# Attention and feed-forward of one kernel interleaved by 256 tokens, on one core

## The chip, the core and the metric

The kernel runs on one core of one Trainium2 chip. The metric is device time in microseconds (us); lower is better. A kernel is executed several times, and medians of its runs are quoted. All runs in this document are of the fast, undisturbed state. The span in a profile is the time from the first to the last instruction of one profiled execution; it is about 2 us shorter than the device time of the same execution.

Names used below: TensorE is PE in the profile (PEld is its weight load), VectorE is DVE, ScalarE is ACT, GpSimd is POOL, SyncE is SP. L289 means line 289 of that kernel's file. PSUM is the accumulator memory that TensorE writes. The granted clock is the share of TensorE's full clock that was let through, as the trace records it. An engine's issue is the distance from the start of one of its instructions to the start of the next.

## The reference, cut to what matters

```
# attention: q, k, v are (4 batches, 8 heads, 768 tokens, 64)
scores = (1 / sqrt(64)) * q @ k.T
scores = where(mask, scores, -1e9)        # blocks of 32: neighbours, first and last block, 3 sampled blocks
attn   = exp(scores - max) / (sum + 1e-9)
x      = attn @ v                         # reordered to 3072 tokens x 512
# feed-forward
h    = x @ w_in                           # 512 -> 1024
e    = exp(h - max);  solu = h * e / (sum(e) + 1e-9)
ln   = (solu - mean) / sqrt(var + 1e-6) * g_ln
out  = ln @ w_out                         # 1024 -> 512
```

Two facts of algebra carry the change. The output of a layer norm does not change (up to the epsilon) when its input is scaled, so the division by the sum of e can be dropped and put into the epsilon (the kernel before does this already). And "subtract the mean, multiply by g, multiply by w_out" is linear, so the subtraction can be folded into the weights once: centred w_out = g * w_out minus the mean of each of its columns. The row factor 1/sqrt(var) can then wait until the output.

## The kernel before

It has two phases. The first does attention, one (batch, head) after the other, and writes x to DRAM. The second reads x back, 128 tokens at a time, and does the feed-forward.

Attention: one head is transposed at a time (64 rows of a 128-row array), scores of 256 columns are collected in tiles of 1536, and ScalarE takes one exponential of each tile.

```
def load_bh_tp(a_tp, bi, qc, kc):
    for src, dst in ((kc, kT), (qc, qT)):
        tp = a_tp.tile([D, S], BF16, tag="tp")
        for c in range(NCH):                                   # 6 transposes of 128 x 64
            nc.tensor.matmul(tp[:, c * TQ : (c + 1) * TQ], src[:, c, :], ident, is_transpose=True, ...)
        nc.vector.tensor_copy(out=dst[0:D, :], in_=tp)
...
    for jh in range(NCH // NJG):                               # 3 tiles a head
        sco = a_sco.tile([TQ, NJG, NSUB, 256], FP32, tag="sco")
        emit_score(jh, qT, kT, sco)                            # 6 matmuls of 256 columns
        if op is not None:
            emit_out(jh, prev_exs, prev_vaug, op, ...)         # attention times v of the head before
        nc.scalar.activation(out=exs[...], in_=sco, func=ACT.Exp, scale=scale)
...
    for ic in range(NCH):                                      # x goes to DRAM
        nc.sync.dma_start(out=x_slabs[b * NCH + ic][:, h * D : (h + 1) * D], in_=o[:, ic, :])
```

Feed-forward, for each 128 tokens:

```
nc.sync.dma_start(out=xt, in_=x_slabs[t])
# 4 transposes of xt into PSUM, then
nc.scalar.copy(out=xT, in_=tps)
# 8 matmuls of 512 columns: hps = x @ w_in
nc.scalar.activation(out=e, in_=hps, func=ACT.Exp, scale=1.0, accum_out=esum)
nc.vector.tensor_mul(out=solu, in0=hps, in1=e)
# bn_stats, bn_aggr: mean and variance; vpe = esum * esum * eps + variance
nc.scalar.activation(out=rstd, in_=vpe, func=ACT.Ln)
nc.scalar.activation(out=rstd, in_=rstd, func=ACT.Exp, scale=-0.5)
nc.vector.tensor_scalar(out=ln, in0=solu, scalar1=mv[:, 0:1], scalar2=rstd, op0=ALU.subtract, op1=ALU.mult)
# 8 transposes of ln into PSUM, then
nc.scalar.copy(out=lnT, in_=tps2)
# 8 matmuls of 512 columns: ops = ln @ w_out
nc.scalar.copy(out=ot, in_=ops)
nc.sync.dma_start(out=out[t * 128 : (t + 1) * 128, :], in_=ot)
```

The softmax here doesn't subtract the row's maximum and nothing guards it: scores larger than these inputs give would overflow.

## Time and profile before

| | before |
|---|---|
| time | 366.1 us median of 4 runs (363.5 to 367.3) |
| attention | about 26 to 177 us; one head takes 4.66 us; its three exponentials of 1.45 us, which overlap a little, keep ScalarE busy for 4.13 us of it (89%) |
| gap between the phases | 177 to 189.5 us |
| feed-forward | 189.5 to 364 us; one tile of 128 tokens takes about 7.3 us |
| ScalarE busy | 277.8 us (76%) |
| TensorE busy | 267.2 us (73%) |

The page of the kernel before, busy time by engine, then the span in 40 slices (a digit is the busy share of a slice in tenths, PEclk the granted clock of TensorE in tenths):

```profile
PE 267.2 (73%) x2772; PEld 180.5 (50%) x2785; DVE 147.3 (40%) x355; ACT 277.8 (76%) x314; POOL 82.8 (23%) x110
...
PE   0049999999999999999356679766867575767654
...
ACT  1018988888888888888429998798878868967883
...
PEclk9999999999999999999769988989898899869888
```

From slice 4 to 19 TensorE is at 9 tenths and ScalarE at 8 to 9. Then comes a hole of one slice, where everything waits for x to go through DRAM. In the second half TensorE is half to three quarters busy, ScalarE is the fuller engine, and the clock is below full.

The page of the kernel before, groups of instructions (busy us, mean ns of one | idle time before them and what ended it):

```profile
L232 ACT ACTIVATE exs<-sco 128x1536 bf16<-128x1536 f32 x96 | 132.4, 1451 | 41.1 <-PE sco L175 41.1
...
L153 PE MATMUL tp<-ident,kc 128*64 128x128 bf16 x192 | 17.5, 229 | 18.9 <-DMA kc<-in_k_dram 18.9
L289 ACT ACT_TABLE_LOAD x24 | 30.8, 1283 | 0.4
...
L290 ACT ACT_TABLE_LOAD x18 | 23.1, 1283 | 0.3
```

Ln and exponential alternate in the feed-forward, and each alternation loads ScalarE's function table again, at 1283 ns. With 6 more before the large exponential there are 48 loads in the second phase, 48 x 1.283 = 61.6 us; one more loads the first table at the very start. The timeline of ScalarE in one feed-forward tile of the kernel before shows them standing right between the work (start, duration):

```profile
302.30 0.58 ACT L264 COPY xT<-tps 128x512 bf16<-128x512 bf16 x1
302.89 1.28 ACT L289 ACT_TABLE_LOAD   x1
304.19 0.20 ACT L289 ACTIVATE rstd<-vpe 128x1 f32<-128x1 f32 x1
304.30 0.57 ACT L264 COPY xT<-tps 128x512 bf16<-128x512 bf16 x1
304.88 1.28 ACT L290 ACT_TABLE_LOAD   x1
306.18 0.20 ACT L290 ACTIVATE rstd<-rstd 128x1 f32<-128x1 f32 x1
```

An activation of 0.20 us costs 1.48 us each time.

The timeline of TensorE in the attention of the kernel before gives the prices that the prediction uses:

```profile
101.16 1.47 PE L175 MATMUL sco<-qT_0_60,kT_0_62 128*128 128x256 bf16 x12
102.47 0.53 PE L185 MATMUL op<-vaug,exs 128*128 128x65 bf16 x12
102.92 0.52 PE L153 MATMUL tp<-ident,kc 128*64 128x128 bf16 x6
```

Twelve matmuls of 256 columns in 1.47 us, of which the last takes 0.27 by itself, are 109 ns from start to start; transposes come out at about 58 ns, attention times v at about 31 ns.

### The profile page before, as it was taken

What the parts mean: (1) busy time and instruction counts of PE and PEld (TensorE: products, weight loads), DVE (VectorE), ACT (ScalarE), POOL (GpSimd) and SP (SyncE); (2) the same over time, 40 slices, a digit from 0 to 9 for tenths busy, and PEclk for the clock granted to TensorE, in tenths of its full rate; (3) what the DMA queues carried; (4) which work ended last, traced back from release to release, by engine and by line L of the source; (5) the groups of instructions that cost most, each with busy time, mean ns of one, the idle gap of its engine ahead of it and who ended that gap; (6) DMA issues with size and microseconds to landing.
All of it is one profiled execution on the core that took longest, in us unless ns stands there. A gap on an engine that the chain in (4) does not pass through costs nothing.

```text
span 364.2 us, 6988 instructions
## 1 busy us (share of the span) xinstructions
PE 267.2 (73%) x2772; PEld 180.5 (50%) x2785; DVE 147.3 (40%) x355; ACT 277.8 (76%) x314; POOL 82.8 (23%) x110
## 2 busy tenths in 40 slices
PE   0049999999999999999356679766867575767654
PEld 0037878888878788888233234333323332323221
DVE  5413343333433343343108454453542615614450
ACT  1018988888888888888429998798878868967883
POOL 4096555555555455510000000000000000000000
PEclk9999999999999999999769988989898899869888
DMA  6699999999999999961121012211120111101011
GB/s 203 143 102 93 86 86 86 85 83 89 88 88 87 86 86 84 89 55 23 23 74 58 31 45 74 98 46 49 66 77 11 58 58 58 46 29 59 12 47 58
DMA packets 112467, 25.64 MB, mean 70 GB/s; under 512 B 104753, under 2 KB 107826, under 8 KB 112434
## 3 DMA queue, kind: packets, MB, share of 16 engines
q0 software_dynamic: 75792, 10.49, 42.2%
q1 hardware_dynamic: 36642, 14.70, 17.6%
q8 instruction: 22, 0.36, 0.4%
q14 instruction: 11, 0.09, 0.1%
HBM read 26.22 MB, written 9.44 MB: 98 GB/s over the span
## 4 chain that ended last, share of the span: by engine, by line
ACT 37%; PE 33%; DVE 10%; DMA 8%; issue 8%; SPq 2%; POOL 0%; ACTq 0%; DVEq 0%
PE sco L175 13%; ACT exs L232 12%; ACT L289 7%; PE ops L303 7%; ACT lnT L300 5%; ACT e L274 4%; PE tp L153 4%; DMA w_out_f<-in_moe_w_out_dram 3%; PE op L185 3%; ACT xT L264 2%; ACT L290 2%; DVE qT_1_61 L156 2%; PE hps L267 2%; PE hps L269 2%; DVE qT_0_60 L156 2%
## 5 line engine op out<-in xcount | busy, mean ns | idle before, releaser
L232 ACT ACTIVATE exs<-sco 128x1536 bf16<-128x1536 f32 x96 | 132.4, 1451 | 41.1 <-PE sco L175 41.1
L303 PE MATMUL ops<-w_out_sb,lnT 128*128 128x512 bf16 x186 | 54.2, 440 | 15.6 <-ACT lnT L300 15.1
L185 PE MATMUL op<-vaug,exs 128*128 128x65 bf16 x1152 | 51.5, 194 | 1.4 <-ACT exs L232 1.2
L277 DVE TENSOR_TENSOR solu<-hps,e 128x1024 bf16<-128x1024 f32 x24 | 29.0, 1210 | 55.8 <-ACT e L274 55.8
L185 PEld LDWEIGHTS <-exs 128*128 128x128 bf16 x1152 | 45.1, 98 | 7.0 <-ACT exs L232 1.5
L267 PE MATMUL hps<-w_in_sb,xT 128*128 128x512 bf16 x94 | 39.6, 421 | 7.1 <-ACT xT L264 6.7
L303 PEld LDWEIGHTS <-lnT 128*128 128x128 bf16 x192 | 19.2, 109 | 47.1 <-ACT lnT L300 23.1
L175 PE MATMUL sco<-qT_0_60,kT_0_62 128*128 128x256 bf16 x288 | 37.8, 278 | 4.6 <-DVE qT_0_60 L156 0.6
L175 PE MATMUL sco<-qT_1_61,kT_1_63 128*128 128x256 bf16 x288 | 36.7, 272 | 4.8 <-ACT exs L232 0.6
L269 PE MATMUL hps<-w_in_sb,xT 128*128 128x512 bf16 x91 | 37.3, 410 | 0.8 <-ACT xT L264 0.8
L141 POOL DMA_DIRECT2D vaug<-in_v_dram x32 | 26.5, 828 | 49.0 <-PE op L185 41.5
L175 PEld LDWEIGHTS <-kT_0_62 128*128 128x128 bf16 x288 | 28.4, 99 | 10.4 <-issue 4.4
L175 PEld LDWEIGHTS <-kT_1_63 128*128 128x128 bf16 x288 | 27.8, 97 | 10.1 <-issue 4.4
L297 PEld LDWEIGHTS <-ln 128*128 128x128 bf16 x192 | 13.1, 107 | 39.3 <-DVE ln L292 36.7
L138 POOL DMA_DIRECT2D qc<-in_q_dram x32 | 26.6, 831 | 24.9 <-PE tp L153 11.9
L153 PE MATMUL tp<-ident,kc 128*64 128x128 bf16 x192 | 17.5, 229 | 18.9 <-DMA kc<-in_k_dram 18.9
L289 ACT ACT_TABLE_LOAD x24 | 30.8, 1283 | 0.4
L292 DVE TENSOR_SCALAR ln<-solu,mv,rstd 128x1024 bf16<-128x1024 bf16 x24 | 13.1, 544 | 42.4 <-ACT rstd L290 42.4
L274 ACT ACTIVATE e<-hps 128x1024 bf16<-128x1024 f32 x24 | 24.6, 1027 | 5.4 <-PE hps L269 5.0
L139 POOL DMA_DIRECT2D kc<-in_k_dram x32 | 26.7, 840 | 0.8 <-PE tp L153 0.6
L306 ACT COPY ot<-ops 128x512 f32<-128x512 f32 x24 | 13.9, 578 | 12.6 <-PE ops L303 12.6
L290 ACT ACT_TABLE_LOAD x18 | 23.1, 1283 | 0.3
(110 smaller groups left out, 276.5 us busy)
## 6 DMA issues: line engine op xcount, KB each, us to landing
out_dram<-ot SPq DMA_DIRECT2D x24, 256.0 KB, 2.0
qc<-in_q_dram POOLq DMA_DIRECT2D x32, 96.0 KB, 3.5
kc<-in_k_dram POOLq DMA_DIRECT2D x32, 96.0 KB, 3.6
vaug<-in_v_dram POOLq DMA_DIRECT2D x32, 96.0 KB, 3.2
w_out_f<-in_moe_w_out_dram SPq DMA_DIRECT2D x1, 2048.0 KB, 11.2
w_in_sb<-in_moe_w_in_dram POOLq DMA_DIRECT2D x1, 1024.0 KB, 10.7
xslab_123<-o SPq DMA_DIRECT2D x8, 16.0 KB, 2.2
xslab_124<-o SPq DMA_DIRECT2D x8, 16.0 KB, 2.5
```

Of the source, the lines that this page charges most:

```text
L139: nc.gpsimd.dma_start(out=kc, in_=k[b, h, :, :].rearrange("(c p) d -> p c d", p=TQ))
L153: nc.tensor.matmul(tp[:, c * TQ : (c + 1) * TQ], src[:, c, :], ident, is_transpose=True, start=(c == 0), stop=(c == NCH - 1))
L175: nc.tensor.matmul(sco[:, jj, c, :], kT[:, jc * TQ : (jc + 1) * TQ], qT[:, c * 256 : (c + 1) * 256], start=(ci % 2 == 0), stop=(ci % 2 == 1))
L185: nc.tensor.matmul(op[:, ic, :], exs[:, jc, ic * TQ : (ic + 1) * TQ], vaug[:, jc, :], start=first, stop=(last and jj == NJG - 1 and ic == ...
L232: nc.scalar.activation(out=exs[:, jh * NJG : (jh + 1) * NJG, :].rearrange("p j (s x) -> p j s x", x=256), in_=sco, func=ACT.Exp, scale=scale)
L267: nc.tensor.matmul(hps[:, 0:512], xT[:, c, :], w_in_sb[:, c, 0:512], start=(c == 0), stop=(c == KD - 1))
L269: nc.tensor.matmul(hps[:, 512:1024], xT[:, c, :], w_in_sb[:, c, 512:1024], start=(c == 0), stop=(c == KD - 1))
L274: nc.scalar.activation(out=e, in_=hps, func=ACT.Exp, scale=1.0, accum_out=esum)
L277: nc.vector.tensor_mul(out=solu, in0=hps, in1=e)
L289: nc.scalar.activation(out=rstd, in_=vpe, func=ACT.Ln)
L290: nc.scalar.activation(out=rstd, in_=rstd, func=ACT.Exp, scale=-0.5)
L303: nc.tensor.matmul(ops, lnT[:, c, :], w_out_sb[:, c, :], start=(c == 0), stop=(c == KF - 1))
```

## The change

The intent is to give ScalarE less to do and to let TensorE work through ScalarE's exponentials. Attention is emitted for 256 queries and all heads, in 12 groups; the feed-forward of one group is cut into pieces that are emitted between the scores of the next group. x stays in SBUF. The feed-forward is transposed: its hidden dimension lies on the partitions, so ln need not be transposed. In both kernels the mask enters the scores as 24 extra rows of the transposed q and k (the mask rows). The sums over the hidden dimension, which now runs over partitions, become one-column matmuls with a vector of ones. The centring is in the weights, the reciprocal square root is a power on GpSimd, and q and k are transposed two heads at a time. The diff, cut to its core:

```diff
-            nc.sync.dma_start(out=xt, in_=x_slabs[t])
-            nc.scalar.copy(out=xT, in_=tps)
+                nc.vector.tensor_copy(out=xT[:, :, qt * P : (qt + 1) * P], in_=tps)
...
-                nc.tensor.matmul(hps[:, 0:512], xT[:, c, :], w_in_sb[:, c, 0:512], ...)
+                    nc.tensor.matmul(h[:, ff, :], w_in_sb[:, c, f * P : (f + 1) * P],
+                                     st["xT"][:, c, :], ...)                     # 32 of 256 columns
+            nc.scalar.activation(out=st["e"][:, sl, :], in_=h, func=ACT.Exp)       # 512 columns
+            nc.vector.tensor_mul(out=st["solu"][:, sl, :], in0=h, in1=st["e"][:, sl, :])
+            nc.vector.tensor_mul(out=st["sq"][:, sl, :], in0=st["solu"][:, sl, :], in1=st["solu"][:, sl, :])
...
-            nc.vector.bn_stats(...); nc.vector.bn_aggr(...)
+                for g, nm in enumerate(("e", "solu", "sq")):
+                    for f in range(KF):
+                        nc.tensor.matmul(s3p[:, qt, g : g + 1],
+                                         st[nm][:, f, qt * P : (qt + 1) * P], onesf[:, 0:1], ...)
...
-            nc.scalar.activation(out=rstd, in_=vpe, func=ACT.Ln)
-            nc.scalar.activation(out=rstd, in_=rstd, func=ACT.Exp, scale=-0.5)
+            nc.gpsimd.tensor_tensor(out=rs, in0=v2, in1=neg_half, op=ALU.pow)
...
-            # ln, 8 transposes of ln, nc.scalar.copy(out=lnT, in_=tps2)
+                nc.tensor.matmul(ops, st["solu"][:, f, qt * P : (qt + 1) * P], w_out_sb[:, f, :], ...)
...
+    def prep_w1():                                       # once, in the first group
+        for c in range(KF):
+            nc.vector.tensor_scalar(out=w_out_g[:, c, :], in0=w_out_f[:, c, :], scalar1=g_sb[:, c : c + 1], ...)
+    def prep_w2():
+        for c in range(KF):
+            nc.tensor.matmul(cs, onesf, w_out_g[:, c, :], ...)
+        nc.scalar.mul(out=wbar, in_=cs, mul=1.0 / d_ff)
+        for c in range(KF):
+            nc.vector.scalar_tensor_tensor(out=w_out_sb[:, c, :], in0=w_out_f[:, c, :],
+                scalar=g_sb[:, c : c + 1], in1=wbar, op0=ALU.mult, op1=ALU.subtract)
...
+    for u, (b, t, pr) in enumerate(units):               # batch, 256 queries, pair of heads
+        for n in range(3):
+            scores(b, t, pr, n, exs)                     # 4 matmuls of 256 columns, exponential of 1024
+            if n == 0 and prev is not None:
+                pv(pb, pt, ppr, pexs, xs[(pb, pt)])      # attention times v of the pair before
+                if ppr == NPR - 1:
+                    bg.extend(ffn_pieces(pb, pt, xs[(pb, pt)]))
+            if bg:
+                bg.popleft()()                           # one piece of background work
```

## The prediction

> **What bounds the kernel now.** The kernel has two phases. By the table of stretches, attention runs from about 25 to 175 us, then the feed-forward from 183 to 364 us; the start is long because the first q/k load waits for w_out scaling (chain of waits: w_out DMA, scaling, load at 17.5 us; first exponential 26.4 us). In attention one head takes 4.66 us, of which ScalarE computes 3 exponentials of 1.45 us: ScalarE bound, 94%. In the feed-forward one 128-token tile takes about 7.5 us and ScalarE is 80-85% busy: exponential 1.03, PSUM copies 0.59, 1.01 and 0.58, and about two table loads of 1.28 us each. TensorE there is busy 70%, at a granted clock near 0.9.
>
> **What the change removes.** All 48 table loads but one (62 us), lnT and xT copies (38 us), half of the output copies (7 us) leave ScalarE; also the 192 transposes of ln, half of the q/k transposes, x's trip through DRAM, bn_stats and the ln pass.
>
> **What it adds.** 576 one-column matmuls for the sums; squares and xT copies on VectorE; mask DMAs at the start; w_out centring once. The attention exponentials become 144 of 1024 columns; 1451 ns at 1536 and 1027 ns at 1024 columns give 0.83 ns a column and 0.18 us fixed, so 148 us instead of 132. Feed-forward exponentials of 512 columns: 48 x 0.60 = 29 us; half of the output 7 us. ScalarE total about 185 us instead of 278.
>
> **New bound: TensorE issue.** Distances between starts read from the timeline of attention: 256 columns 109 ns (12 in 1.47 us), attention-times-v 31 ns, transposes 58 ns, 512 columns 217 ns. The Trainium skill, "TensorE: Matmul & The Clock Gate", section "Back-to-back issue gap", gives N/2.4 + 2.5 ns, 109 ns for 256: this trace agrees. The sums I take at 31 ns too, an estimate (same page: never below about 25 ns). Per group of 256 tokens: scores 48 x 109 = 5.2; a.v 96 x 31 = 3.0; h 32 x 109 = 3.5; sums 1.5; output 16 x 217 = 3.5; x transposes 0.5; q/k transposes 0.9 on average: 18.1 us, against 15.3 us of ScalarE. Eight of twelve slots carry feed-forward work and are TensorE bound, four are exponential bound: 18.6 us, with the coupling loss of 5% seen now T = 19.5 us per group; VectorE needs about 12 us.
>
> **Time.** First exponential about 20 us (VectorE: memsets, mask, copies in order). The first group has no feed-forward but VectorE is loaded with transposes' copies and 16 w_out operations: ends near 39 us. 11 groups x 19.5 = 214. The last feed-forward runs alone: about 11 us. Sum 264 us; range 247 to 284. Faster by over 2%: 0.98; within 2%: 0.015; slower: 0.005.
>
> **What would show it.** One table load; ScalarE busy about 185 us (70%); TensorE clock near 1.0 in the middle and its busy tenths all 9; distance of group starts 19-20 us; waits of exponentials for scores where feed-forward runs; one-column matmuls every 25-35 ns; the chain mostly TensorE lines (scores, h, output, sums).
>
> **What would make it wrong.** One-column matmuls at 60 ns or more (+1.5 us per group, +16 us); GpSimd's power chain being slow, holding the two-buffer PSUM pool (+1-2 us per group); GpSimd loads blocking that chain; a start longer than 25 us from VectorE or mask DMAs; or better overlap than assumed, T near 18 us (248 us).

## The result, and the profile after

Ratios here and below are the mean time of one kernel's fast runs over the mean time of the kernel before's fast runs of the same rounds, so they are not quite the ratio of the medians that stand beside them.

| | before | after |
|---|---|---|
| time, median | 366.1 us | 281.95 us (281.8 to 282.8, 4 runs) |
| ratio | | 0.772, 95% interval 0.769 to 0.775 |
| ScalarE busy | 277.8 us | 174.4 us (62%) |
| TensorE busy | 267.2 us | 238.8 us (85%) |
| table loads | 49 | 1 |
| mean granted clock | 0.932 | 0.997 |

The change takes 84 us off. The predicted 264 us is 18 us below the result; the result lies inside the range, near its upper end.

The page of the kernel after, in the same order as before:

```profile
PE 238.8 (85%) x3163; PEld 183.2 (65%) x3177; DVE 157.9 (56%) x365; ACT 174.4 (62%) x206; POOL 82.8 (29%) x142
...
PE   0116686999999999999999999999999999899783
...
ACT  1002468548858859667677688588488595785630
...
PEclk9999999999999999999999999999999999999998
```

From slice 8 on, up to the last slices, TensorE is at 9 of 10 almost without a break; ScalarE is at 4 to 9. The engines have changed places. Beyond that, two things stand out: the first seven slices, about 50 us, are not full, and neither are the last three.

The timeline of TensorE in the steady part of the kernel after:

```profile
170.12 1.91 PE L268 MATMUL h<-xT,w_in_sb 128*128 128x256 bf16 x16
...
177.13 0.34 PE L283 MATMUL s3p<-onesf,e 128*128 128x1 bf16 x8
...
178.12 1.89 PE L304 MATMUL ops<-w_out_sb,solu 128*128 128x512 bf16 x7
...
182.34 0.50 PE L161 MATMUL tp<-ident,kc 128*128 128x128 bf16 x6
```

Eight one-column matmuls take 0.34 us, of which the last is 0.164 by itself: (0.34 - 0.164) / 7 = 25 ns from start to start. The Trainium skill, "TensorE: Matmul & The Clock Gate", section "Wait — 56ns, not 53.3ns?", says that start-to-start never goes below about 25 ns, however few the columns; this trace agrees, and the 31 ns of the prediction were a little too careful.

The timeline of ScalarE in the kernel after, the first feed-forward exponential of the first two groups and of the last two:

```profile
52.83 0.60 ACT L272 ACTIVATE e<-h 128x512 bf16<-128x512 f32 x1 [0.36 <-PE h L268]
...
72.30 0.60 ACT L272 ACTIVATE e<-h 128x512 bf16<-128x512 f32 x1 [0.43 <-PE h L268]
...
249.73 1.30 ACT L272 ACTIVATE e<-h 128x512 bf16<-128x512 f32 x2
...
268.44 0.60 ACT L272 ACTIVATE e<-h 128x512 bf16<-128x512 f32 x1 [3.36 <-PE h L268]
```

From 52.83 to 249.73 there are ten groups, so one takes 19.7 us. The prediction said 19.5. What is wrong lies outside: the first group and the last.

To see the first group, read VectorE, which works through its queue in order. That order is the compiled one and not quite that of the program: the copies into va_92, the v of the second batch, belong to later units than the w_out work and still stand ahead of part of it. The timeline of VectorE in the kernel after, some lines up to the first feed-forward work (in brackets, the idle time before and what ended it):

```profile
15.27 0.63 DVE L167 COPY va_91<-vc 128x768 bf16<-128x768 bf16 x1 [11.16 <-DMA vc<-in_v_dram]
...
34.14 3.80 DVE L192 TENSOR_SCALAR w_out_g<-w_out_f,g_sb 128x512 bf16<-128x512 f32 x8
...
42.49 0.52 DVE L167 COPY va_92<-vc 128x768 bf16<-128x768 bf16 x1 [0.93 <-DMA vc<-in_v_dram]
42.93 5.37 DVE L203 SCALAR_TENSOR_TENSOR w_out_sb<-w_out_f,g_sb,wbar 128x512 bf16<-128x512 f32 x8
...
48.55 0.76 DVE L240 TENSOR_TENSOR x<-op,r 128x256 bf16<-128x256 f32 x2
...
50.19 0.42 DVE L240 TENSOR_TENSOR x<-op,r 128x256 bf16<-128x256 f32 x1
```

VectorE waits 11.16 us for the first v although the work on the mask, which the first scores need, stands behind that copy. Later a copy of the second batch's v and the 9.2 us on w_out (3.80 + 5.37) stand ahead of the norms of the first group (the divisions that write x), which end at 50.6 us. The first batch's own last data, the v of its fourth pair, had landed at 32.2 us; from 20 to 50 us VectorE is busy for 26.2 of the 30 us (table of stretches).

The timeline of TensorE in the kernel after, the same instructions early and a little later:

```profile
24.37 0.80 PE L161 MATMUL tp<-ident,qc 128*128 128x128 bf16 x6 [1.53 <-DVE qT_87 L166]
...
34.19 1.53 PE L231 MATMUL op<-va_91,ex 128*128 128x65 bf16 x24
...
38.98 0.49 PE L161 MATMUL tp<-ident,qc 128*128 128x128 bf16 x6
...
41.29 0.91 PE L231 MATMUL op<-va_91,ex 128*128 128x65 bf16 x24
```

Until about 36 us the same six transposes take 0.80 us instead of 0.49, and the same 24 matmuls 1.53 us instead of 0.91: TensorE runs at about half rate up to then. The prediction did not count this either.

The last group's feed-forward has no attention beside it to hide in. The timeline of all engines at the end of the kernel after:

```profile
265.81 0.42 DVE L240 TENSOR_TENSOR x<-op,r 128x256 bf16<-128x256 f32 x1
...
267.37 1.91 PE L268 MATMUL h<-xT,w_in_sb 128*128 128x256 bf16 x16 [0.62 <-DVE xT L258]
...
274.87 0.17 DVE L290 TENSOR_TENSOR s_4734<-s3p,st_sel 128x6 f32<-128x6 f32 x1 [1.07 <-PE s3p L283]
...
275.93 0.69 POOL L298 TENSOR_TENSOR rs<-v_4738,neg_half 128x2 f32<-128x2 f32 x1
...
277.15 0.69 ACT L312 ACTIVATE ot<-ops,rs 128x512 f32<-128x512 f32 x1 [4.53 <-PE ops L304]
```

From the last division, which ends at 266.2 us, to the end at 281.1 us there are 14.9 us: 1.2 us for transposing x, 7.5 us for h, exponentials, products and sums in turns, 1.8 us up to the end of the power, 1.2 us up to the end of the last output tile, and 3.3 us until it has left.

### The profile page after: what moved, and what is told of

The parts are those of the page before. It is cut to its first block, busy times and chain, and to the rows that moved or that the text cites. A ratio compares the mean times of both kernels' runs of the same rounds, so it can differ in the third digit from the quotient of the medians.

```text
span 281.1 us, 7445 instructions
## 1 busy us (share of the span) xinstructions
PE 238.8 (85%) x3163; PEld 183.2 (65%) x3177; DVE 157.9 (56%) x365; ACT 174.4 (62%) x206; POOL 82.8 (29%) x142
## 2 busy tenths in 40 slices
DMA packets 61636, 20.40 MB, mean 73 GB/s; under 512 B 52225, under 2 KB 56994, under 8 KB 61602
## 4 chain that ended last, share of the span: by engine, by line
PE 62%; DMA 11%; ACT 10%; DVE 9%; issue 3%; POOL 3%; ACTq 0%; POOLq 0%
PE s L215 15%; PE h L268 15%; PE ops L304 14%; PE op L231 10%; ACT ex L220 8%; DMA kc<-in_k_dram 7%; PE s3p L283 6%; DMA vc<-in_v_dram 4%; DVE w_out_sb L203 2%; ACT ot L312 2%; PE tp L161 2%; POOL qc L73 1%; DVE xT L258 1%; PE tps L256 1%; DVE x L240 1%
## 5 line engine op out<-in xcount | busy, mean ns | idle before, releaser
L220 ACT ACTIVATE ex<-s 128x1024 bf16<-128x1024 f32 x144 | 141.1, 1024 | 68.9 <-PE s L215 67.8
L215 PE MATMUL s<-qT_87,kT_85 88*128 88x256 bf16 (+1 forms) x288 | 49.5, 284 | 5.8 <-ACT ex L220 3.1
L231 PEld LDWEIGHTS <-ex 128*128 128x128 bf16 x1152 | 45.7, 98 | 11.1 <-ACT ex L220 4.6
L268 PE MATMUL h<-xT,w_in_sb 128*128 128x256 bf16 x384 | 47.8, 272 | 1.3 <-DVE xT L258 0.6
L215 PE MATMUL s<-qT_88,kT_86 88*128 88x256 bf16 (+1 forms) x288 | 46.2, 272 | 2.0 <-ACT ex L220 1.2
L273 DVE TENSOR_TENSOR solu<-h,e 128x512 bf16<-128x512 f32 x48 | 33.0, 687 | 26.3 <-ACT e L272 26.2
L304 PE MATMUL ops<-w_out_sb,solu 128*128 128x512 bf16 x179 | 44.6, 378 | 0.9 <-DVE s_4734 L290 0.3
L268 PEld LDWEIGHTS <-w_in_sb 128*128 128x128 bf16 x384 | 37.0, 97 | 6.3 <-issue 1.6
L272 ACT ACTIVATE e<-h 128x512 bf16<-128x512 f32 x48 | 28.7, 598 | 18.1 <-PE h L268 16.9
L215 PEld LDWEIGHTS <-kT_85 88*128 88x128 bf16 (+1 forms) x288 | 27.3, 101 | 13.5 <-issue 6.0
L215 PEld LDWEIGHTS <-kT_86 88*128 88x128 bf16 (+1 forms) x288 | 26.0, 97 | 9.3 <-issue 4.0
L73 POOL DMA_DIRECT2D qc<-in_q_dram x32 | 26.2, 822 | 8.0 <-DMA w_in_sb<-in_moe_w_in_dram 3.7
L231 PE MATMUL op<-va_92,ex 128*128 128x65 bf16 x576 | 26.2, 193 | 2.7 <-ACT ex L220 2.2
L231 PE MATMUL op<-va_91,ex 128*128 128x65 bf16 x576 | 25.2, 196 | 1.9 <-DVE x L240 1.0
L274 DVE TENSOR_TENSOR sq<-solu 128x512 bf16<-128x512 bf16 x48 | 20.4, 425 | 1.3
```

The source lines that it names most:

```text
L73: nc.gpsimd.dma_start(out=t[:, :, hh, :], in_=src[b, 2 * pr + hh, :, :].rearrange("(p c) d -> p c d", p=P))
L215: nc.tensor.matmul(s[:, m, :], kT[i][rows[hh], hh, pr, jc * P : (jc + 1) * P], qT[i][rows[hh], hh, pr, t * TW : (t + 1) * TW], start=(m % ...
L220: nc.scalar.activation(out=e, in_=s, func=ACT.Exp, scale=scale)
L231: nc.tensor.matmul(op[:, qt, hh, :], exs[n][:, m, qt * P : (qt + 1) * P], va[i][:, 2 * pr + hh, jc, :], start=first, stop=(n == 2 and m == ...
L268: nc.tensor.matmul(h[:, ff, :], w_in_sb[:, c, f * P : (f + 1) * P], st["xT"][:, c, :], start=(ff == 0 and c == 0), stop=(ff == 1 and c == ...
L272: nc.scalar.activation(out=st["e"][:, sl, :], in_=h, func=ACT.Exp)
```

## The experiments

All runs but one gave correct results. Each was run in three rounds against the kernel before.

### Where the 84 us came from

**e1: the kernel before without table switches.** Only the Ln and the exponential of the reciprocal root are replaced by a power on GpSimd.

```diff
-            nc.scalar.activation(out=rstd, in_=vpe, func=ACT.Ln)
-            nc.scalar.activation(out=rstd, in_=rstd, func=ACT.Exp, scale=-0.5)
+            nc.gpsimd.tensor_tensor(out=rstd, in0=vpe, in1=neg_half, op=ALU.pow)
```

> The kernel before with one edit: the reciprocal root of the variance is taken by GpSimd's power instruction instead of ScalarE's logarithm and exponential, so that no activation table is switched. Theory A (the table switches, 48 of 1.28 us in ScalarE's stream, are the largest single part of the feed-forward phase): one 128-token tile falls from 7.5 us to about 5 us, where TensorE (about 4.2 us of issue) takes over; total about 306 us. Rival B (the feed-forward phase is bound by the chain through four engines and by the TensorE clock that drops in the gaps): total 335 us or more. Correct result either way, one table load, ScalarE busy about 62 us less.

Measured: 329.6 us, ratio 0.901 (0.895 to 0.906). ScalarE falls from 277.8 to 209.1 us busy. So 36 us are gained of the 62 us that the loads took: the time lies between the two expectations, nearer to B's. From one tile's exponential to the next there are 5.4 us on average in the trace of e1, 6.7 in that of the kernel before. From 190 to 318 us TensorE is now the fullest engine (busy 102 of 128 us), then VectorE (80) and ScalarE (72). Taking the largest item off an engine does not give its whole time when other engines and the waits between them come close behind.

**e2: the kernel after, but in two phases.** All feed-forward pieces are emitted after all attention; x has twelve buffers instead of two.

```diff
-                if ppr == NPR - 1:
-                    bg.extend(ffn_pieces(pb, pt, xs[(pb, pt)]))
...
+    for key in sorted(xs):
+        for piece in ffn_pieces(key[0], key[1], xs[key]):
+            piece()
```

> The changed kernel with its feed-forward pieces emitted after the whole attention instead of between its steps (x of all twelve groups stays in SBUF). Theory A (interleaving is what makes TensorE full, since attention alone is bound by ScalarE and feed-forward alone by its chain): attention 26 + 48 x 3.2 = about 180 us, feed-forward 12 x 10 to 13 us, total 300 to 335 us. Rival B (the gain comes from the work removed, the order matters little): under 290 us.

Measured: 321.2 us, ratio 0.877 (0.871 to 0.883). The page of e2, ScalarE's busy tenths:

```profile
ACT  1004674999999999999999622312322322231230
```

ScalarE is full in the first half and at 2 to 3 tenths in most of the second, and theory A's 300 to 335 us came true. The interleaving is worth 321.2 - 282.0 = 39 us. The runs form a ladder: table switches 366 to 330, everything else but the interleaving 330 to 321, the interleaving 321 to 282. These three steps add up to the 84 us by construction; in another order the shares would differ.

### Is TensorE's issue the bound in the steady part?

**e4: one of eight chunks summed.** This removes 504 of the 576 one-column matmuls. The result is wrong (relative error 7).

```diff
-                    for f in range(KF):
+                    for f in range(1):
```

> The changed kernel with the sums taken over one of eight chunks: 6 one-column matmuls per group instead of 48 (wrong result on purpose). Theory A (TensorE's issue is the bound in the steady part, one-column matmuls come every 25 ns): 42 x 25 ns x 12 = 12.6 us less, total about 269 us. Rival B (they fill TensorE waits that exist anyway): under 4 us less.

Measured: 270.5 us, ratio 0.741 (0.736 to 0.745), 11.4 us less. 504 matmuls at 25 ns are 12.6 us. In the trace of e4 ten of the eleven distances from group to group are 0.95 to 0.97 us shorter than in the kernel after, 23 ns for each of the 42 matmuls removed. The removed issue time comes back almost whole, although each is only a one-column matmul.

**e5: q and k transposed twice.** This adds 192 transposes, as many as the change saves by pairing heads, into the same PSUM tile.

```diff
+            for rep in range(2):
                 for c in range(NCH):
                     nc.tensor.matmul(tp[:, c * P : (c + 1) * P], src[:, c, :, :], ident, is_transpose=True, ...)
```

> The changed kernel with every q/k transpose issued twice into the same tile: 192 more transposes on TensorE, nothing else. Theory A (TensorE issue is the bound once feed-forward runs; 48 of the transposes fall in the start, where it is not): 144 x 58 ns = 8.4 us more, at most 11 us; so pairing the transposes, which saved 192, is worth about the same. Rival B (they sit in waits): under 3 us.

Measured: 293.2 us, ratio 0.802 (0.798 to 0.806), 11.2 us more, about the expectation's upper limit. That 192 x 58 ns = 11.1 us is the same is a coincidence. In the trace of e5 the 48 transposes of the start cost nothing (the first feed-forward exponential comes at 51.3 us, 52.8 in the kernel after). The six distances from group to group that contain the other 144 are 1.74 to 1.85 us longer, 10.8 us together, 75 ns a transpose; the others are unchanged. The transposes themselves still start 56 ns apart; the rest is in short waits of TensorE, for ScalarE and VectorE, which grow from 3.6 to 7.1 us between 60 and 250 us. So TensorE's issue is the bound, but an added transpose costs a third more than its issue. That the pairing of the transposes is worth about as much in the interleaved kernel is inferred from this.

### Where the missing 18 us are: the start

The first exponential comes at 26.1 us instead of the predicted 20, the first feed-forward exponential at 52.8. Can the start be shortened by rearranging? Eight runs tried. In the table, all in us: the first attention exponential, the first feed-forward exponential of the first two groups and of the last (from the timeline of ScalarE of each), and the median time.

| run | first exp. | group 1 | group 2 | group 12 | time |
|---|---|---|---|---|---|
| after | 26.1 | 52.8 | 72.3 | 268.4 | 281.95 |
| e3 both weights late | 19.9 | 47.8 | 75.4 | 271.0 | 285.2 |
| e7 w_out after the mask | 19.5 | 56.0 | 74.4 | 271.3 | 286.0 |
| e8 as e7, first v copy on ScalarE | 17.2 | 58.9 | 77.3 | 273.5 | 286.2 |
| e9 as e8, w_in later | 17.0 | 57.8 | 76.2 | 272.3 | 287.5 |
| e10 longer packets | 24.0 | 50.0 | 70.4 | 270.0 | 285.7 |
| e11 as e10, weights late | 14.6 | 52.8 | 72.7 | 271.1 | 285.9 |
| e12 w_out off VectorE | 25.2 | 48.1 | 76.8 | 273.6 | 288.9 |
| e13 w_out also off GpSimd | 25.9 | 49.3 | 69.2 | 265.3 | 280.5 |

**e3: both weight loads late.** They go to GpSimd's queue behind the four head pairs of the first batch; the preparation of w_out moves to units 4 and 5.

```diff
-        nc.sync.dma_start(out=w_out_f, in_=moe_w_out...)
+        nc.gpsimd.dma_start(out=w_out_f, in_=moe_w_out...)
-        if pr == 1:
+        if pr == 3:
```

> The changed kernel with w_in and w_out loaded on the GpSimd queue after all four pairs of the first batch, and the scaling and centring of w_out done at the fifth and sixth step instead of the second and third. Theory A (the late start, first exponential at 26 us instead of the predicted 20, and first feed-forward at 52 us instead of 41, comes from the 2 MB of w_out and 2 MB of w_in competing with the first q/k/v): first exponential at 17 to 20 us, total 270 to 275 us. Rival B (VectorE's order of memsets, mask and copies sets the start): first exponential later than 23 us, total above 278 us.

Measured: 285.2 us, ratio 0.780 (0.775 to 0.785). The first exponential comes 6 us earlier, but w_out lands only at 38.9 us, VectorE waits 3.85 us for it, and the second group comes 3 us later than in the kernel after. The expected gain on the total was missed.

**e7: w_out loaded after the mask.** The load is made to depend on the mask rows by a copy of one element.

```diff
+    nc.vector.tensor_copy(out=w_out_f[0:NB, 0, 0:1], in_=mskp[:, 0, 0:1])
+    nc.sync.dma_start(out=w_out_f, in_=moe_w_out...)
-        if u == 1:
+        if u == 3:                                        # prep_w1; prep_w2 at u == 4
```

> The changed kernel with the w_out load held back until the mask rows exist (a one-element copy from the mask into its tile orders it), on its own queue, and its scaling and centring at the fourth and fifth step. Theory A (the earlier run with both weights late lost its gain because w_out landed at 39 us behind w_in and VectorE waited for it with the normalisations behind): first exponential at about 20 us, w_out landed by 33 us, total 273 to 277 us. Rival B (the first 45 us are bound by the sum of all transfers, whatever their order): first feed-forward exponential still at 50 us or later, total 280 us or more.

Measured: 286.0 us, ratio 0.784 (0.780 to 0.788); the rival's case. VectorE waits 8.39 us for the v of the fourth pair, which lands at 37.9 us.

**e8: e7, and the first v copy on ScalarE**, so that VectorE is not held up by the first v (11.16 us in the kernel after, 4.92 us in e7).

```diff
+        if b == 0 and pr == 0:
+            nc.scalar.copy(out=va[i][:, 2 * pr : 2 * pr + 2, :, 0:D], in_=vc)
```

> As the run with w_out after the mask, and the first copy of v is made by ScalarE, which is idle then, instead of standing ahead of the mask work in VectorE's order. Theory A (VectorE's order is the second cause of the late start): first exponential at about 15 us, total 3 to 5 us below the run with w_out after the mask. Rival B: transfers bind after that, under 1.5 us less.

Measured: 286.2 us, ratio 0.784 (0.779 to 0.790); the rival's case. The timeline of TensorE in e8 shows where the early start ends:

```profile
18.30 1.01 PE L217 MATMUL s<-qT,kT 128*128 128x256 bf16 x4 [0.26 <-ACT ex L222]
29.57 0.80 PE L161 MATMUL tp<-ident,kc 128*128 128x128 bf16 x6 [10.26 <-DMA kc<-in_k_dram]
```

After some seven microseconds of early work TensorE stands still for 10.26 us: k of the third head pair is not there yet. It was issued by 14.4 us and lands at 29.4 us, while w_in and then w_out come in beside it.

**e9: e8, and w_in behind the third pair.**

```diff
-        if pr == 1:
+        if pr == 2:
             load_weights()
```

> As the run before it, with w_in loaded after the third pair of the first batch instead of the second. Theory A (w_in holds up the third pair of q/k/v): 1 to 4 us less than the run before it. Rival B (w_in becomes the late one, first feed-forward waits): equal or slower.

Measured: 287.5 us, ratio 0.788 (0.784 to 0.792). The gap moves, and grows to 14.2 us.

**e10: longer packets.** q and k are loaded with the head outermost, in packets of 1536 bytes instead of shorter ones, and the transposes pair two chunks of tokens instead of two heads.

```diff
-            t = ld.tile([P, NCH, 2, D], BF16, tag=nm, name=nm)
+            t = ld.tile([P, 2, NCH, D], BF16, tag=nm, name=nm)
...
-            nc.vector.tensor_copy(out=dst[0:D, 0, pr, :], in_=tp[0:D, :])
-            nc.vector.tensor_copy(out=dst[D:P, 1, pr, :], in_=tp[D:P, :])
+            for hh in range(2):
+                for w in range(2):                        # four copies of half the size
+                    nc.vector.tensor_copy(out=dv[:, :, w, :], in_=tpv[w * D : (w + 1) * D, hh, :, :])
```

> The changed kernel with q and k loaded for two heads with the head outermost in the tile, so that a packet reads 1536 bytes instead of 256, and each transpose pairs two token chunks of one head instead of two heads (same 192 transposes; VectorE's copies become four of 64x384 instead of two of 64x768 per tile). Theory A (the first 45 us are bound by the DMA engines, and there by the number of small packets, about 37 ns for one on one engine as the changed kernel's trace has it; the period of 19.6 us per group is TensorE's and stays): first feed-forward exponential at 42 to 48 us instead of 52.8, total 273 to 278 us. Rival B (bytes bind, not packets): total 280 to 284 us.

Measured: 285.7 us, ratio 0.785 (0.782 to 0.787). Packets fall from 61,636 to 20,164, and the second group comes 1.9 us earlier. But a group with transposes in it now takes 20.4 to 21.1 us instead of 19.5 to 20.5, and the last group comes 1.6 us later. A gain at the start was paid for in the steady part, and the total lies above both expectations. VectorE has four smaller copies in place of two there (busy 164.8 instead of 157.9 us); that they are the cause is likely, but not shown. (A form that kept one copy per half by a transpose over both heads did not build and never ran.)

**e11: e10 with the late weights of e3 and the first v copy on ScalarE.** (The edits are those of e10, e3 and e8 together, with the preparation at unit 4.)

> As the run with token pairs, with both weights loaded on the GpSimd queue after the first batch, w_out prepared at the fifth step, and the first copy of v made by ScalarE. Theory A (with fewer packets the later weights still come in time): first exponential at about 15 us, first feed-forward exponential at 38 to 45 us, total 265 to 273 us. Rival B (as in the earlier late-weight runs, the waits only move): no gain over the run with token pairs.

Measured: 285.9 us, ratio 0.784 (0.782 to 0.786). The first exponential comes at 14.6 us, 11.5 us earlier than in the kernel after, and the second group 0.4 us later than there: VectorE waits 7.86 us for w_out.

**e12: the preparation of w_out off VectorE.** The product with g goes to ScalarE, the subtraction to GpSimd. (A first form, with the fused operation on GpSimd, did not compile and never ran.)

```diff
-            nc.vector.tensor_scalar(out=w_out_g[:, c, :], in0=w_out_f[:, c, :], scalar1=g_sb[:, c : c + 1], ...)
+            nc.scalar.activation(out=w_out_g[:, c, :], in_=w_out_f[:, c, :], func=ACT.Copy, scale=g_sb[:, c : c + 1])
...
-            nc.vector.scalar_tensor_tensor(out=w_out_sb[:, c, :], ..., op0=ALU.mult, op1=ALU.subtract)
+            nc.gpsimd.tensor_sub(out=w_out_sb[:, c, :], in0=w_out_g[:, c, :], in1=wbar)
```

> The changed kernel, loads as they were, with the preparation of w_out taken off VectorE: the scaling by ScalarE, which idles until the first exponential, the centring as a subtraction on GpSimd from the scaled copy. Theory A (the first feed-forward starts at 52.8 us in spite of earlier data in five runs because 9 us of w_out work stand in VectorE's order ahead of the normalisations of the first attention group): first feed-forward exponential at 42 to 46 us, periods of 19.6 us unchanged, total 271 to 276 us. Rival B (the transfers or the mask bind the first 50 us): first feed-forward exponential later than 50 us, total above 279 us.

Measured: 288.9 us, ratio 0.792 (0.787 to 0.796). The first feed-forward exponential does come 4.7 us earlier. Then, in the timeline of all engines of e12:

```profile
39.81 9.12 POOL L202 TENSOR_TENSOR w_out_sb<-w_out_g,wbar 128x512 bf16<-128x512 bf16 x8 [2.25 <-ACT wbar L200]
...
54.35 0.36 DVE L167 COPY va<-vc 128x768 bf16<-128x768 bf16 x1 [7.69 <-DMA vc<-in_v_dram]
...
56.53 1.86 PE L265 MATMUL h<-xT,w_in_sb 128*128 128x256 bf16 x8 [7.00 <-DVE solu L270]
```

GpSimd also issues the loads, in order. For 9.12 us it subtracts and issues nothing; the v loads of the next batch come late; VectorE's copy of that v stands in order ahead of the products of the feed-forward, and TensorE waits 7.00 us. The subtraction itself costs 1.14 us per 128x512. The Trainium skill, "GPSIMD Engine Reference", section "Performance versus the Vector engine", gives 4497 ns for an addition of 2048 float32 elements, from which 1.12 us for 512 is an estimate by proportion; the trace's 1.14 us is close to it.

**e13: w_out off VectorE and off GpSimd.** ScalarE does the products, before its first exponential; TensorE does the centring as two accumulating matmuls a chunk, and ScalarE copies the results out.

```diff
+            nc.scalar.activation(out=w_out_g[:, c, :], in_=w_out_f[:, c, :], func=ACT.Copy, scale=g_sb[:, c : c + 1])
...
-        nc.scalar.mul(out=wbar, in_=cs, mul=1.0 / d_ff)
+        nc.scalar.mul(out=wbar, in_=cs, mul=-1.0 / d_ff)
...
+            wc = ps_h.tile([P, d_model], FP32, tag="h", name="wc")
+            nc.tensor.matmul(wc, ident, w_out_g[:, c, :], start=True, stop=False)
+            nc.tensor.matmul(wc, ident, wbar, start=False, stop=True)
+            nc.scalar.copy(out=w_out_sb[:, c, :], in_=wc)
...
-        if u == 1:                                        # prep_w1
+        if u == 0:                                        # prep_w1 and prep_w2
```

> The changed kernel with the preparation of w_out off both VectorE and GpSimd: the products w_out times g go to ScalarE, which has nothing to do before the first exponentials; the centring is done by TensorE, as two accumulating matmuls a chunk (identity times the product, identity times minus the column mean), and ScalarE copies the eight results out of PSUM. Theory A: the run with the centring on GpSimd showed the first feed-forward exponential at 48.1 instead of 52.8 us, and lost it because GpSimd's 9.1 us of centring held back the issue of the next batch's v loads, for which VectorE's in-order v copies then waited 7.7 us. With both engines free, the first feed-forward exponential comes at 45 to 48 us, no wait of several us for a v load follows, and the total is 273 to 277 us, a ratio near 0.755. Rival B: as in the earlier attempts the wait moves on to the next in-order queue, the second group again starts at 72 us or later and the total is 280 us or more.

Measured: 280.5 us, ratio 0.768 (0.766 to 0.771), against 281.95 us and 0.772 (0.769 to 0.775) for the kernel after. The mechanism of theory A held: the wait of several us is gone, and from the second group on all groups come 3.1 us earlier in the profiled executions (the fastest of e13's runs beside the slowest of the kernel after's). The size did not: the first feed-forward exponential comes at 49.3 us, not 45 to 48, and the total, above A's 273 to 277 us and at the edge of B's "280 us or more", is 1.5 us lower by the medians. The intervals of the two ratios still overlap a little, so this is the best kernel that was run, by an amount at the edge of what these runs can tell. The timeline of TensorE in e13 shows a second benefit:

```profile
27.90 2.77 PE L198 MATMUL cs<-w_out_g,onesf 128*128 128x512 bf16 x8
30.51 0.50 PE L161 MATMUL tp<-ident,kc 128*128 128x128 bf16 x6
```

The dense matmuls for the column means now stand in the sparse work of the start, and from 30.5 us on the transposes take 0.50 us; in the kernel after, they took 0.80 or more until 36 us. What each of the two benefits is worth was not separated.

### Why an earlier first exponential did not shorten the kernel

Two causes can be read from these runs. First, in each of e3, e7, e8, e9, e11 and e12 an in-order queue stood still for one transfer: 3.85 us (e3, w_out), 8.39 (e7, v), 10.26 (e8, k), 15.16 (e9, v), 7.86 (e11, w_out) and 7.69 (e12, v of the next batch). In the kernel after, transfers run at 185 to 198 GB/s from 10 to 40 us (table of stretches, which counts bytes as they land, so q, k, v and w_in as bf16). Counted so, q, k and v of the first batch (2.4 MB) and the two weight matrices (3.1 MB) are 5.5 MB, which need 29 us at 190 GB/s; this is an estimate from the sizes and that rate, and the first batch's last v lands at 32.2 us. In these runs, what was moved to the front pushed back something else that the first group or its feed-forward also needed. But by 40 us 7.5 MB have landed: besides the mask rows, the loads of the second batch, which GpSimd issues from 26.5 us on, share the transfers, and the v of theirs that lands at 42.5 us stands ahead of w_out work in VectorE's queue. No run held these loads back, so whether that would shorten the start is not tested.

Second, an interrupted TensorE runs slowly afterwards. The table of stretches of e9, in columns of 10 us (length, busy us of PE, PEld, DVE, ACT and POOL, granted clock, DMA share, GB/s):

```profile
20.00:30.00 10.00, 2.53 (x40) 1.76 (x37) 3.29 (x7) 3.23 (x4) 3.18 (x5) 0.82 1.11 248
30.00:40.00 10.00, 1.92 (x13) 1.38 (x14) 1.34 (x3) 1.02 (x1) 4.01 (x6) 0.50 1.94 207
40.00:50.00 10.00, 9.93 (x121) 7.71 (x119) 8.41 (x21) 6.58 (x8) 7.96 (x10) 0.83 1.86 178
50.00:60.00 10.00, 8.21 (x75) 6.22 (x74) 7.29 (x16) 7.77 (x9) 1.43 (x2) 0.83 0.51 71
```

TensorE starts early, stands still for 14 us, is granted half its clock, and is busy at 0.83 for the 20 us after that. The Trainium skill, "TensorE: Matmul & The Clock Gate", section "HAM oscillation — how this bites in real kernels", says that idle gaps of TensorE of more than about 3.4 us must be avoided, because the clock gate then halves the rate. These runs agree as far as they go. In e3, e7, e8, e9, e11 and e12 TensorE stood still for 4.2 to 14.2 us once work had begun, and each profile has stretches of lowered clock before 65 us; in the kernel after and in e13 no single wait of TensorE between 20 and 262 us reaches 2 us, and the recorded clock stays at 1.00 up to the tail. A long gap is not the only way to a lower clock, though: in e4 no wait of TensorE between 25 and 70 us exceeds 2.56 us, and the clock still reads 0.50 from 31 to 34 us and from 48 to 51 us. e8 shows the effect in one kernel: its four runs had mean clocks of 0.982, 0.988, 0.993 and 1.000 and spans of 287.0, 285.4, 283.6 and 282.9 us. No run takes the gap away and leaves all else, so how the loss divides between the wait and the slow clock after it stays open.

## Why the prediction was right or wrong, point by point

- **The bound moves to TensorE's issue: right.** TensorE's tenths are 9 through the middle, the clock is 0.997, 62% of the chain that ended last (followed back from the last instruction through what each one waited for) is TensorE, ScalarE's exponentials wait 67.8 us for scores (24.0 of them before the first), and e4 and e5 change the time about as the issue of the instructions says: a tenth less for e4, a third more for e5's transposes in the steady part.
- **A group takes 19.5 us: right.** Measured 19.7 us over ten groups. The one-column matmuls cost 25 ns, not 31, which makes the predicted sum 0.3 us smaller; what comes on top of it is then 1.4 us and not the assumed 0.9. Two small errors partly cancel here.
- **ScalarE about 185 us, one table load: right, with a difference of reading.** The durations add up to 144 x 1.024 + 48 x 0.598 + 12 x 0.687 = 184 us. The busy time is 174.4 us, because neighbouring instructions overlap and busy time counts the overlap once. The busy share is 62%, not 70%.
- **The power on GpSimd as a risk: did not come true.** It takes 0.69 us, its chain about 1.5 us, and it holds nothing up in the steady part.
- **"First exponential about 20 us", "the first group ... ends near 39 us": wrong, and the largest part of the error.** The first group's last division ends at 50.6 us, 11.6 us later. The prediction named "a start longer than 25 us from VectorE or mask DMAs" as a risk, and the first exponential came at 26.1 us. But it took VectorE's list of work as if all data were there, and as too short. In its place the runs showed VectorE waiting 11.16 us for the first v, then busy for 26.2 of the 30 us from 20 to 50 us with 9.2 us of w_out work in it, a copy of the second batch's v (landed at 42.5 us) ahead of part of that work in its queue, and TensorE at half rate until about 36 us. Without the w_out work on VectorE (e13) the first feed-forward exponential came 3.5 us earlier; what the other parts are worth stays open.
- **"11 groups x 19.5 = 214": mis-sized by 1.6 us.** From the last division of group 1 (50.6) to that of group 12 (266.2) there are 215.6 us.
- **"The last feed-forward runs alone: about 11 us": too small by 3.9 us.** It took 14.9 us. This is read from the trace; no run tested it. The sum 11.6 + 1.6 + 3.9 = 17.1 is the distance from 264 to the profiled span of 281.1 us.

## What to carry to other kernels

When two phases are bound by different engines, running one inside the other can be worth more than shortening either: here 39 us, a little more than the 36 us of removing all table switches. Once an engine's issue is the bound, its instructions can be priced from start to start: here the distance of the groups was predicted within a few per cent, but the cost of one added or removed kind of instruction only within a tenth (e4) to a third (e5); the start and the tail need their own sum, in which each in-order queue waits for its latest input. In these runs starting the busiest engine earlier did not help where it could not go on without a gap: a start that is later but dense (e13) beat starts that were up to 11 us earlier and interrupted.

## What the Trainium skill lacked or had wrong

- "TensorE: Matmul & The Clock Gate", section "Part 4: PE-mode transpose", gives about 275 ns for a 128x128 transpose in a kernel's context and says that the full clock does not engage for transposes. In the steady part here one takes 216 to 219 ns and six take 0.50 us together, about 56 ns from start to start; in the sparse start one takes 314 ns and six 0.80 us, so they do follow the clock.
- "ScalarE: Activation LUTs", section "What ACT_TABLE_LOAD costs": the 1283 ns of a load are confirmed (mean 1283 ns, 49 loads). The extra 1380 ns that it counts for a drain at each switch do not show: here the loads stand directly between neighbours (302.89 to 304.17 us, the next activation at 304.19).
- "ScalarE: Activation LUTs", section "Table sets: the hidden batching unit", says that one set holds exponential and logarithm, so that one load would do. In the kernel before, 24 tiles that alternate the two made 48 loads.
- No page gives the time of a power on GpSimd: 0.55 us for 128x1 (e1) and 0.69 us for 128x2 (after).
- No page says that a record of the granted clock can read full before its first change: in the kernel after it reads 1.00 in the first 36 us, while the durations there are those of about half rate (1.53 against 0.91 us for the same 24 matmuls).
